# Strided sparse attention and a Mish MLP on one core: holding Pool's loads until the last transposed piece has landed, in every block

## The chip, the cores and the metric

The kernel runs on one core of one Trainium2 chip. The metric is device time in microseconds (us), lower is better. Before the change the median of three runs is 288.06 us (287.17 to 288.32).

## The reference

Attention over 8 batches of 8 heads, with 576 positions of 64 values, and then an MLP over all 4608 tokens. In four heads a position sees itself and the 31 positions before it (local); in the other four it sees the earlier positions that are congruent to it modulo 32 (strided).

```python
# q, k, v: 8 x 8 x 576 x 64 float32; w_in: 512 x 2048, w_out: 2048 x 512
scores = (q @ k.T) / sqrt(64)
rel = pos[:, None] - pos[None, :]
mask_local = (rel >= 0) & (rel < 32)                                   # heads 0 to 3
mask_strided = (rel >= 0) & (pos[None, :] % 32 == pos[:, None] % 32)   # heads 4 to 7
attn = softmax(where(mask, scores, -1e9))
x = (attn @ v)          # heads side by side: 4608 tokens x 512
h = x @ w_in
out = (h * tanh(softplus(h))) @ w_out
```

## The kernel before

**Blocks.** The 4608 tokens go through the MLP in nine blocks of 512 (t = 0 to 8), while attention goes by batch (576 tokens, b = 0 to 7). Block t computes the MLP of its 512 tokens and, woven into its second half, the attention of batch t+1; the attended tokens go into a ring `xT` of four batches. At the same time it brings in the data of batch t+2. The order on every engine is written out by hand: what is called first is queued first on its engine, and each engine works through its queue in order, waiting where an operand isn't there.

**One block** (t from 1 to 7). `mlp1` gives seven steps: `begin`, `second`, `third`, `fourth`, a group of matmuls, `fifth`, `end`. They form the first product and Mish, by a scheme with seven products of halves instead of eight. Then `mlp2_seven` gives 14 steps for the second product. After step i of these the list `at[i]` is called, with the attention of batch t+1:

- `at[0]`: `load_qk_str(t+2)`, the strided k and q of batch t+2 (tiles `ks`, `qs`), on Pool's queue.
- `at[1]`: the strided scores and the last part of the local scores (matmuls of line 333, which read the transposed `qTs`, `kTs`, `qTl`, `kTl`).
- `at[3]` and `at[5]`: masks of the local scores on Pool (line 353), the rest of the local scores, the first strided products with v.
- `at[7]`: ACT copies the rows of local v that neighbouring windows share (`share_v_loc`, line 181).
- `at[10]` to `at[12]`: the local products with v (line 369), and the transposes into `xT`.

**How a batch's q and k get transposed.** The strided ones are loaded by Pool's DMAs with a cast. The local ones come as float32 by SP's DMAs (`load_qk_loc`, line 140, tiles `kl32` and `ql32`), issued at the end of the block before, and Pool casts them after step 9 (`cast_qk_loc`, line 199). Then `transpose_by_dma(t+2)` queues six DMA transposes on SP after step 10: kTs, qTs (line 224), and kTl, qTl for each of two pairs of heads (line 230). The last is qTl of the second pair. They are used in the middle of the next block. Behind them on SP stand the two stores of the block's output (line 744), the DMA transposes of the tail of `xT` (line 445), and the next float32 loads.

**How v gets in.** Local v of batch t+1 is loaded in step `fourth` of block t by four DMAs on Pool's queue (`load_own_v_loc`, line 175, tile `vl`). Strided v of batch t+2 follows (`load_early_v_str`, line 154, tile `vsr`) and is spread by VectorE at the beginning of the next block. All of `load_own_v_loc`, `load_early_v_str` and `load_qk_str` are plain waits-and-issues in Pool's queue, so they stand one after the other there, behind the casts of the block before and ahead of the masks of this block.

**The mark.** In block 1 alone, Pool first copies four elements of the last transposed piece, `qTl[0:1, 1, S - 4:S]`, into a tile `mark` that nothing reads (line 628). Since the copy reads what the last DMA transpose writes, Pool waits there until that transpose has landed, and its loads are issued only then.

Of the kernel before, what the change touches and what calls it, by code (L numbers as in the profile page):

```python
# [43 lines left out]
def kernel(ctx, tc, q, k, v, moe_w_in, moe_w_out, out):  # L44
    nc = tc.nc
    B, H, S, D = q.shape
# [106 lines left out]
    def load_early_v_str(b):  # L153
        nc.gpsimd.dma_start(vs_raw(), v[b, 4:8].rearrange("h (p j) d -> p h (j d)", j=CS))
# [18 lines left out]
    def load_own_v_loc(b):  # L173
        for h in range(4):
            nc.gpsimd.dma_start(  # L175
                vl[b % 2][32:128, :, h, 0:D], v[b, h].rearrange("(w p) d -> p w d", p=WQ)
            )
# [328 lines left out]
    def mlp1(t, accs):  # L506
# [41 lines left out]
        def product(ps, f0, lhs, rhs, first=False, last=False):  # L548
            for n, p in enumerate(ps):
                for j in range(2):  # L550
                    f = f0 + 256 * n + 128 * j
                    for cc in range(2):
                        nc.tensor.matmul(  # L553
                            p[:, 256 * j:256 * j + 256], lhsT=lhs[:, cc, f:f + 128],
                            rhs=rhs[:, cc], start=(first and j == 0 and cc == 0),
                            stop=(last and cc == 1), skip_group_check=True,
                        )

        def mish(src, half_f, half_t, c0):
            src = src.rearrange("p (j n) -> p j n", n=256)  # L560
            c = 8 * half_f + c0
            nc.scalar.activation(  # L562
                gT[:, c:c + src.shape[1], 256 * half_t:256 * half_t + 256], src, AF.Mish,
            )
# [54 lines left out]
        def fourth():  # L619
            product(z[2], 0, a22, t4, last=True)  # L620
            for n in range(2):
                mish(z[2][n], 1, 0, 2 * n)
            if t == 1:
                sums_w()[2](slice(4, 8))
                sums_w()[3](slice(0, 4))
            sums_g(gT, 0, 4, "12")
            if t == 1:
                Po.tensor_copy(mark[:], qTl[0:1, 1, S - 4:S])
            if t < B - 1:
                load_own_v_loc(t + 1)  # L630
            if t < B - 2:
                load_early_v_str(t + 2)
# [9 lines left out]
        def end():  # L642
# [9 lines left out]
            sums_g(gT, 7, 8, "12")  # L652

        return gT, z, [begin, second, third, fourth, lambda: group(6), fifth, end]

    def sums(out_, in0, in1, op):
        nc.vector.tensor_tensor(out=out_, in0=in0, in1=in1, op=op)  # L657

    def sums_g(gT, c0, c1, which="1234"):

        lo1, lo2 = gT[:, c0:c1, 0:256], gT[:, c0:c1, 256:512]
        hi1, hi2 = gT[:, 8 + c0:8 + c1, 0:256], gT[:, 8 + c0:8 + c1, 256:512]
        s1, s2, s4 = [Sg[:, i, c0:c1, :] for i in range(3)]
        if "1" in which:
            sums(s1, lo2, hi2, ALU.add)
        if "2" in which:
            sums(s2, s1, lo1, ALU.subtract)
        if "3" in which:
            sums(lo2, lo1, lo2, ALU.subtract)
        if "4" in which:  # L670
            sums(s4, hi1, s2, ALU.subtract)
# [5 lines left out]
    def sums_w():  # L677

        b11, b12 = w_out[:, 0:8, 0:256], w_out[:, 0:8, 256:512]
        b21, b22 = w_out[:, 8:16, 0:256], w_out[:, 8:16, 256:512]  # L680
        return [
            lambda c: sums(tw_of(0)[:, c], b12[:, c], b11[:, c], ALU.subtract),
            lambda c: sums(tw_of(1)[:, c], b22[:, c], tw_of(0)[:, c], ALU.subtract),
            lambda c: sums(b12[:, c], b22[:, c], b12[:, c], ALU.subtract),
            lambda c: sums(tw_of(3)[:, c], b21[:, c], tw_of(1)[:, c], ALU.subtract),
        ]
# [364 lines left out]
```

## Time and profile before

| | before |
|---|---|
| median of 3 runs | 288.06 us (287.17 to 288.32) |
| profiled execution | 290.55 us |
| its span | 288.8 us |
| granted TensorE clock, mean | 0.993 |
| PE, PEld, DVE, ACT, POOL busy | 97%, 76%, 66%, 68%, 36% |
| DMA, mean over the span | 141 GB/s |

The span runs from the first to the last instruction of the profiled execution; its time holds some 1.75 us more around that. Busy shares are averages over the whole span, so the prediction cuts the span into blocks. PE is the matmul engine, PEld its weight loads, DVE VectorE, ACT ScalarE, POOL GpSimd, and SPq the queue of SyncE, which only issues DMAs. For an SPq row, the time is that of the issue; the landing is told separately. A DMA share above 1 means that packets of several queues were in flight on the same engines.

### The profile page before, as it was taken

The numbers are of one execution on the slowest core, as the hardware profiler recorded it, in microseconds if no ns is written. First come the engines' busy times: TensorE is split into PE (matmuls) and PEld (weight loads), VectorE is DVE, ScalarE is ACT, GpSimd is POOL, SyncE is SP. The second block draws the span as 40 slices with busy tenths as digits, with TensorE's granted clock in tenths as the row PEclk, the third lists the DMA queues.
The fourth block names the chain that finished last, engine by engine and source line by source line (L and its number), as shares of the span: only waits on it lengthen the run. The fifth ranks groups of instructions, "written<-read, shape, count | busy, mean of one in ns | idle before, by whom it ended". The sixth has DMA issues, their size and how long they took to land.

```text
span 288.8 us, 7515 instructions
## 1 busy us (share of the span) xinstructions
PE 279.3 (97%) x3106; PEld 219.3 (76%) x3121; DVE 190.8 (66%) x403; ACT 196.6 (68%) x292; POOL 105.3 (36%) x122
## 2 busy tenths in 40 slices
PE   8999999999999969999999999999999999999995
PEld 3564455686898648977898889778977897788684
DVE  2273167889786737768776777687868776735742
ACT  2578643699857947689758985898589858506920
POOL 8375536307396015910691069306710600000000
PEclk9999999999999979999999999999999999999999
DMA  8999999999979999999999999999993032003004
GB/s 158 185 205 190 193 194 199 145 137 241 171 102 116 130 257 160 144 235 152 161 109 123 218 151 139 143 227 151 160 149 113 1 137 47 0 3 145 0 2 145
DMA packets 103965, 40.73 MB, mean 141 GB/s; under 512 B 86396, under 2 KB 99436, under 8 KB 103932
## 3 DMA queue, kind: packets, MB, share of 16 engines
q1 hardware_dynamic: 67900, 25.13, 57.1%
q0 software_dynamic: 35744, 14.87, 46.8%
q8 instruction: 24, 0.39, 0.6%
q10 hardware_dynamic: 288, 0.25, 0.3%
q14 instruction: 9, 0.07, 0.1%
HBM read 37.20 MB, written 9.44 MB: 162 GB/s over the span
## 4 chain that ended last, share of the span: by engine, by line
PE 87%; DMA 7%; DVE 2%; ACT 1%; POOL 1%; issue 1%; SPq 0%; ACTq 0%; POOLq 0%
PE pso L749 30%; PE psu L553 10%; PE psh L522 9%; PE psv L553 8%; PE psb L553 7%; PE po L369 4%; PE pso L809 4%; PE psb L522 4%; PE pso L782 4%; DMA qTl<-ql 4%; DMA ql<-in_q_dram 4%; PE ps L333 3%; PE trx L418 1%; PE tr L267 1%; DVE x_l L381 1%
## 5 line engine op out<-in xcount | busy, mean ns | idle before, releaser
L353 POOL TENSOR_TENSOR Pl<-Pl,consts_sb 128x960 bf16<-128x960 bf16 (+1 forms) x18 | 29.2, 1635 | 87.1 <-issue 68.5
L749 PEld LDWEIGHTS <-gT 128*128 128x128 bf16 x448 | 41.8, 98 | 5.8
L553 PEld LDWEIGHTS <-w_in 128*128 128x128 bf16 x384 | 37.4, 98 | 8.5
L749 PE MATMUL pso<-w_out,gT 128*128 128x256 bf16 x336 | 40.9, 273 | 0.0
L749 PEld LDWEIGHTS <-Sg 128*128 128x128 bf16 x336 | 32.1, 100 | 5.1
L522 PEld LDWEIGHTS <-w_in 128*128 128x128 bf16 x208 | 20.3, 98 | 16.7 <-issue 0.6
L553 PEld LDWEIGHTS <-Sw 128*128 128x128 bf16 x288 | 28.2, 98 | 3.3
L522 PE MATMUL psh<-xT,w_in 128*128 128x512 bf16 (+1 forms) x127 | 29.0, 365 | 0.8 <-ACT xT L197 0.2
L749 PE MATMUL pso<-Tw,Sg 128*128 128x256 bf16 x224 | 28.0, 281 | 0.0
L197 ACT COPY xT<-trx 128x576 bf16<-128x576 bf16 (+3 forms) x24 | 14.2, 629 | 18.4 <-PE trx L418 13.0
L197 ACT COPY osb<-pso 128x512 f32<-128x512 f32 (+1 forms) x17 | 9.4, 554 | 22.3 <-PE pso L749 12.9
L562 ACT ACTIVATE gT<-psu 128x1024 bf16<-128x1024 f32 x16 | 16.4, 1025 | 8.4 <-PE psu L553 8.4
L657 DVE TENSOR_TENSOR psu<-psb,p 128x512 f32<-128x512 f32 x16 | 11.2, 700 | 13.8 <-PE psb L553 13.0
L395 DVE TENSOR_TENSOR x_s<-po,rden 72x512 bf16<-72x512 f32 x28 | 19.2, 687 | 1.0
L175 POOL DMA_DIRECT2D vl<-in_v_dram x24 | 18.8, 791 | 0.5 <-PE psv L553 0.4
L533 ACT ACTIVATE gT<-psh 128x1024 bf16<-128x1024 f32 x16 | 16.2, 1024 | 3.9 <-PE psh L522 3.8
L657 DVE TENSOR_TENSOR Sg<-gT 128x256 bf16<-128x256 bf16 (+2 forms) x32 | 12.8, 421 | 8.0 <-ACT gT L562 6.7
L553 PE MATMUL psu<-xT,w_in 128*128 128x256 bf16 x128 | 17.9, 272 | 0.0
L347 ACT ACTIVATE Ps<-ps 72x864 bf16<-72x864 f32 (+1 forms) x18 | 14.7, 857 | 4.6 <-PE ps L333 4.6
L726 DVE TENSOR_TENSOR p<-pso,p 128x512 f32<-128x512 f32 x14 | 9.6, 685 | 12.1 <-PE pso L749 12.1
L553 PE MATMUL psb<-Sx,w_in 128*128 128x256 bf16 x128 | 17.2, 272 | 0.0
L522 PE MATMUL psb<-xT,w_in 128*128 128x512 bf16 (+1 forms) x72 | 16.4, 355 | 0.0
(139 smaller groups left out, 593.2 us busy)
## 6 DMA issues: line engine op xcount, KB each, us to landing
out_dram<-osb SPq DMA_DIRECT2D x9, 512.0 KB, 8.0
out_dram<-p SPq DMA_DIRECT2D x7, 512.0 KB, 6.7
kl<-in_k_dram SPq DMA_DIRECT2D x5, 576.0 KB, 10.2
ql<-in_q_dram SPq DMA_DIRECT2D x5, 576.0 KB, 14.2
qs<-in_q_dram POOLq DMA_DIRECT2D x8, 288.0 KB, 13.4
vsr<-in_v_dram POOLq DMA_DIRECT2D x8, 288.0 KB, 9.4
w_in<-in_moe_w_in_dram POOLq DMA_DIRECT2D x4, 512.0 KB, 9.6
w_out<-in_moe_w_out_dram POOLq DMA_DIRECT2D x4, 512.0 KB, 17.9
```

Source lines behind the costliest of these rows:

```text
L175: nc.gpsimd.dma_start(vl[b % 2][32:128, :, h, 0:D], v[b, h].rearrange("(w p) d -> p w d", p=WQ))
L197: nc.scalar.copy(out_, in_)
L347: nc.scalar.activation(pt[0:n, :, 0:nw], ps[0:n, :, o0:o0 + nw], AF.Exp, scale=scale)
L353: meng.tensor_tensor(out=pm, in0=pm, in1=mk[0:n, :].unsqueeze(1).unsqueeze(1).to_broadcast([n, 2, nu, w]), op=ALU.mult,)
L369: nc.tensor.matmul(po[:, h, :], lhsT=pt[0:n, c0:c0 + 128], rhs=rhs, start=True, stop=True,)
L395: nc.vector.tensor_tensor(out=dst.rearrange("p e (h d) -> p e h d", h=4), in0=po[0:m, :, :, 0:D], in1=rden[0:m].unsqueeze(3).to_broadcast( ...
L522: nc.tensor.matmul(ps_u[:, o:o + n], lhsT=w_in[:, cc, fc * 128:(fc + 1) * 128], rhs=xT[:, cc, a:a + n], start=(cc == 2 and (o == 0 or len( ...
L533: nc.scalar.activation(to, tiles[g][:], AF.Mish)
L553: nc.tensor.matmul(p[:, 256 * j:256 * j + 256], lhsT=lhs[:, cc, f:f + 128], rhs=rhs[:, cc], start=(first and j == 0 and cc == 0), stop=(la ...
L562: nc.scalar.activation(gT[:, c:c + src.shape[1], 256 * half_t:256 * half_t + 256], src, AF.Mish,)
L657: nc.vector.tensor_tensor(out=out_, in0=in0, in1=in1, op=op)
L749: nc.tensor.matmul(ps[:, pair, :], lhsT=lhs(c, 128 * pair), rhs=rhs(c), start=(first and pair == 0 and c == 0), stop=(last and c == 7), sk ...
```

## The change

The copy into `mark`, and with it the wait for the last transposed piece, is done in every block in which local v is loaded (t = 1 to 6), not only in block 1. The loads themselves, their order and their sizes are the same.

```diff
             sums_g(gT, 0, 4, "12")
-            if t == 1:
+            if t < B - 1:
                 Po.tensor_copy(mark[:], qTl[0:1, 1, S - 4:S])
-            if t < B - 1:
                 load_own_v_loc(t + 1)
             if t < B - 2:
                 load_early_v_str(t + 2)
```

## The prediction

> **What bounds the kernel now.** I read the page first, then the busy time of the seven steady blocks (stretches cut where PE starts a block's first product), then the waits, the chain, and the Pool and SP queues in order of time.
>
> ```profile
> span 288.8 us, 7515 instructions
> PE 279.3 (97%) x3106; PEld 219.3 (76%) x3121; DVE 190.8 (66%) x403; ACT 196.6 (68%) x292; POOL 105.3 (36%) x122
> ...
> 57.40:86.46 29.06, 29.01 (x350) 24.40 (x349) 24.97 (x50) 24.23 (x36) 14.34 (x16) 1.00 1.24 162
> 86.46:119.90 33.44, 30.72 (x349) 25.26 (x349) 21.49 (x44) 23.40 (x35) 13.92 (x16) 0.95 1.36 164
> 119.90:148.88 28.98, 28.93 (x347) 24.30 (x347) 21.42 (x44) 23.02 (x35) 13.13 (x15) 1.00 1.27 166
> 148.88:177.81 28.93, 28.93 (x362) 25.79 (x361) 21.41 (x44) 22.88 (x35) 12.60 (x14) 1.00 1.43 158
> 177.81:206.71 28.90, 28.85 (x346) 24.21 (x345) 21.51 (x44) 22.86 (x35) 12.12 (x14) 1.00 1.40 163
> 206.71:235.51 28.80, 28.75 (x343) 24.14 (x343) 21.93 (x44) 22.70 (x35) 8.87 (x9) 1.00 0.58 99
> ...
> PE ps L333 <- DMA qTl<-ql: 2.7, 2, 1.5
> ...
> 93.96 10.47 DMA qTl<-ql
> ```
>
> The columns of a stretch are its length, the busy time of PE, PEld, DVE, ACT and POOL, the granted clock, the DMA share and GB/s. These are blocks 1 to 6. PE sets the time: blocks 3 to 6 are 28.8 to 29.0 us of PE without a gap. Only block 2 is longer, 33.44 us. Against block 3 that is **4.46 us**: PE is idle for 2.72 us (33.44 less 30.72) instead of 0.05, and busy 1.79 us longer under a granted clock of 0.95. The wait row and the chain name the cause: the score matmuls L333 waited 2.7 us for transposed pieces of q, the last of which was issued at 93.96 and landed 10.47 us later, at 104.43. So a DMA wait of PE costs 4.46 / 2.67 = 1.67 times its length here. The other blocks have no PE time to win; they can only lose.
>
> **What the change removes.** Block 1 has the hold already, block 2 doesn't. The two show what company does to the last transpose.
>
> ```profile
> L230 SPq DMA_TRANSPOSE qTl<-ql x1: 1210/1210/1210, 62.7 to 62.7; - x1
> DMA to landing us min/median/max: 3.0/3.0/3.0
> ...
> L230 SPq DMA_TRANSPOSE qTl<-ql x1: 2812/2812/2812, 94.0 to 94.0; - x1
> DMA to landing us min/median/max: 10.5/10.5/10.5
> ...
> 65.84 0.71 POOL L628 COPY mark<-qTl 1x4 bf16<-1x4 bf16 x1 [11.46 <-DMA qTl<-ql]
> 66.50 0.72 POOL L175 DMA_DIRECT2D vl<-in_v_dram  x1
> 70.64 0.72 POOL L126 DMA_DIRECT2D ks<-in_k_dram  x1
> 71.35 0.70 POOL L126 DMA_DIRECT2D qs<-in_q_dram  x1
> 85.77 3.25 POOL L175 DMA_DIRECT2D vl<-in_v_dram  x4
> ...
> 50.99 1.44 SPq L224 DMA_TRANSPOSE kTs<-ks  x1
> 84.00 1.44 SPq L224 DMA_TRANSPOSE kTs<-ks  x1
> 85.84 1.78 SPq L224 DMA_TRANSPOSE qTs<-qs  x1
> 206.12 1.22 SPq L230 DMA_TRANSPOSE kTl<-kl  x1
> 210.07 1.25 SPq L230 DMA_TRANSPOSE qTl<-ql  x1
> ```
>
> With Pool's loads held the last piece landed in 3.0 us, with four vl loads and more started at 85.77 it took 10.5. Held in block 2 too, the six transposes (one DMA each for kTs and qTs, two each for kTl and qTl) start at 84.00 as before and run alone. Their length alone is in no row. Low: kTs and qTs are issued by 85.84 + 1.78 = 87.6, four local pieces take 3.95 us from first to last issue (206.12 to 210.07), the last lands in 3.0: 94.6, or 10.6 us. High: the set of 50.99 to 65.84, 14.8 us, whose issues were spaced wider. I take 11.5, nearer to the low row, because block 2's casts are done when Pool goes on to vl at 85.77; the landing is then 95.5. The score matmuls need the last piece 15.2 us into a block (row 163.42 below, from 148.88), that is at 101.7. **Block 2's loss goes: 4.46 us in the profiled execution.** That execution took 290.55 us with a span of 288.8, 1.75 around it; the median of the shown runs is 288.06, 2.49 less. If all of that lies in block 2's wait, the gain in an ordinary run is 4.46 - 2.49 = 1.97. I keep 1.97 and 4.46 as its ends and sum with 4.46.
>
> The Trainium skill, page "DMA: Bandwidth & Descriptors", section "Queues, rings and completion order", says that each DMA engine takes turns between the queues that have work, packet by packet. An estimate by that page: two queues sharing evenly double a transfer, so block 2's set of 20.4 us in company would take 10.2 alone and every cycle below would be 1.3 us shorter; the traced 3.0 against 10.5 is worse than double, so I don't build on it.
>
> **What it adds.** Per block one 0.71 us copy on Pool, and a wait in front of it. Queued behind it on Pool are four vl loads, one vsr load (block 6: vl alone), ks and qs, and behind those the masks of the local scores and the casts of kl and ql. Nothing is behind it on SP. The wait is never free: the last transpose needs the ql cast that stands just ahead of the mark on the same queue.
>
> ```profile
> 137.57 0.91 POOL L353 TENSOR_TENSOR Pl<-Pl,consts_sb 128x384 bf16<-128x384 bf16 x1 [13.66 <-issue]
> 140.67 3.96 POOL L353 TENSOR_TENSOR Pl<-Pl,consts_sb 128x960 bf16<-128x960 bf16 x2 [2.19 <-ACT Pl L347]
> 163.42 0.71 PE ps L333 x36
> 171.85 1.26 ACT L181 COPY vl<-vl 32x1280 bf16<-32x1280 bf16 x1
> 173.56 0.42 PE L369 MATMUL po<-vl,Pl 128*128 128x65 bf16 x8
> ...
> L175 POOL DMA_DIRECT2D vl<-in_v_dram x4: 725/725/734, 66.5 to 69.2; - x4
> DMA to landing us min/median/max: 6.8/7.1/9.8
> ...
> L126 POOL DMA_DIRECT2D ks<-in_k_dram x1: 720/720/720, 70.6 to 70.6; - x1
> DMA to landing us min/median/max: 13.3/13.3/13.3
> ...
> L175 POOL DMA_DIRECT2D vl<-in_v_dram x4: 725/762/815, 207.7 to 210.0; - x4
> DMA to landing us min/median/max: 5.5/6.0/6.7
> ...
> 98.53 3.95 SPq L445 DMA_TRANSPOSE xT<-x_l  x2
> 185.18 5.77 SPq L445 DMA_TRANSPOSE xT<-x_l  x4
> ```
>
> Call m the landing of the last piece. *Masks.* Pool has issued all loads 72.05 - 65.84 = 6.2 us after m; its first mask is due 17.7 us into a block (137.57 from 119.90), so up to m = +11.5 (11.5 us into its block) the 13.66 us of idle time cover the delay. Beyond that two masks (0.91 + 1.98) must end by +24.7, where local PV starts (173.56 from 148.88): m up to +15.6. *Local v.* In block 1 the slowest vl landing is bounded by 66.50 + 9.8 = 76.3, m + 10.5. ACT then shares rows (1.26 us) before PV at +24.7, so vl must be there at +23.4: **m up to +12.9**, tighter than the scores' +15.2. In block 6, with less to load, the limit is 23.4 - (0.7 + 2.3 + 6.7) = +13.7.
>
> *The next set.* ks is issued 4.8 us after m, lands 13.3 later, and only then does SP start the next set: 84.00 - 65.84 = 18.2 us from m in block 1. So the hold closes a loop: m, loads, landing, transposes, next m. Its length is 18.2 + 11.5 = 29.7 us, plus what the transposes of xT cost, which block 1 doesn't send. Two took SP's queue 3.95 us, four 5.77; bounds are 0 and their mean, 4.9; local pieces, leaving SP every 1.3 us, suggest less than half of that, and I take 2.0. **Cycle: 31.7 us against a block of 28.9.** Ends: 28.8 (10.6 and 0) and 37.9 (14.8 and 4.9).
>
> *The sum.* Blocks start at 86.46, then (less 4.46) 115.44, 144.42, 173.35, 202.25. m is 95.5 (+9.0), 127.2 (+11.8), 158.9 (+14.5, 1.6 too late, times 1.67 = 2.7 us); block 5 then starts at 176.05, m is 190.6 (+14.55, costs 2.75); block 6 starts at 207.7, m is 222.3 (+14.6, 0.9 too late, costs 1.5). Lost 6.95, won 4.46: **+2.5 us, 290.6 us** on the median.
>
> **The rivals.**
>
> *Faster: the work of the DMA engines is only reordered.* Before, last pieces still landed well in most blocks, and the DMA share of 1.27 to 1.43 in blocks 3 to 5 says that the engines were busy in company anyway. If the transposes run so much faster alone that they give back what the loads lose, the cycle stays at or below 30.1, m in block 6 is at or below 215.9 (+13.7) and no block waits. The gain is 1.97 to 4.46, 283.6 to 286.1; I put it at 284.6. It decides at a cycle of 30.1, only 0.4 above the sum without xT. The Trainium skill, "DMA: Bandwidth & Descriptors", section "Issuing engines are not separate DMA queues", speaks for it: all queues run on the same 16 engines and interleave. Against it stands the gap that the hold leaves, 18.2 us in which no transpose can start.
>
> *Cancelled out.* At a cycle of 31.3 the same working loses 1.3 + 3.1 + 0.6 = 5.0 and wins 4.46: within 0.5% of before. About 30.9 to 31.5 gives this; 288.
>
> *Much slower.* At a cycle of 33, m is +13.1, +16.8, +14.4, +16.0: lost 0.25 + 6.5 + 2.5 + 3.8 = 13.0, net +8.6, 296.6. For it: xT's 3.95 to 5.77 us on SP stand whole in the cycle.
>
> That the hold does nothing can be left out, by the order of cast and mark on Pool.
>
> **How the numbers follow.** The cycle decides: 0.32 for the reorder, 0.14 for cancelled out, 0.40 for the forecast, 0.14 for much slower. A measurement here can tell about 0.5%, 1.44 us. So faster 0.32, same 0.14, slower 0.54. The range goes from 284.4, into the reorder's gain, to 296.0, short of the far case; the forecast's own range is 289.5 to 294.
>
> **What would show it.** In the profile after: block 2 is 29 us, its last qTl lands in 3 to 5 us near 95.5, and the mark starts there; marks follow at distances of about 31.7 us; SP's kTs transposes start about 18 us after each mark; in blocks 4 to 6 ACT's L181 or PE's L369 waits for vl, in the later ones perhaps L333 for qTl as well. Marks every 30 us or less, each under 12.9 us into its block, and blocks of 28.9 throughout would prove me wrong, as would vl loads that land within 7 us after the mark.

## Result and the profile after

The changed kernel takes 286.81 us (median of six runs, 286.68 to 287.23), the kernel before 288.19 in the same comparison (287.17 to 288.96): a ratio of **0.9954, 95% interval 0.9932 to 0.9977**. It is faster by 1.4 us, where 2.5 us slower was forecast. In a second comparison the ratio was 0.9962 (0.9929 to 0.9994). The ratios leave out executions that lie more than 1.5% above the fastest of their kernel, which here only kernels had whose profiles show PE waiting; medians and ranges in this text are over all executions.

The profiled execution took 286.68 us with a span of 284.8, 4.0 less than the span before. The same cut into blocks 1 to 6 as in the prediction (columns as there):

```profile
57.55:86.60 29.05, 29.05 (x350) 24.38 (x349) 24.95 (x50) 24.24 (x36) 13.65 (x15) 1.00 1.23 168
86.60:115.67 29.07, 29.07 (x351) 24.40 (x349) 21.50 (x44) 23.18 (x35) 12.73 (x15) 1.00 1.24 169
115.67:144.65 28.98, 28.98 (x348) 24.32 (x347) 21.89 (x44) 23.02 (x35) 13.41 (x15) 1.00 1.17 163
144.65:173.58 28.93, 28.93 (x362) 25.78 (x361) 22.22 (x44) 22.88 (x35) 13.01 (x15) 1.00 1.32 159
173.58:202.47 28.89, 28.89 (x347) 24.20 (x345) 22.76 (x44) 22.86 (x35) 13.80 (x15) 1.00 1.22 166
202.47:231.28 28.81, 28.81 (x345) 24.16 (x343) 21.41 (x44) 22.70 (x35) 9.61 (x10) 1.00 0.71 113
```

Block 2 is 29.07 us, 4.37 less than in the profile before. PE is busy for the whole of every block and its clock is 1.00 throughout; the waits of PE for qTl are gone, and no new one has come. Pool's queue shows the marks, and the ks load behind the first of them; SP's queue shows the starts of the next sets, and the last load of ql ahead of one of them:

```profile
65.98 0.72 POOL L628 COPY mark<-qTl 1x4 bf16<-1x4 bf16 x1 [10.47 <-DMA qTl<-ql]
70.76 0.72 POOL L126 DMA_DIRECT2D ks<-in_k_dram  x1
94.33 0.18 POOL L628 COPY mark<-qTl 1x4 bf16<-1x4 bf16 x1 [9.04 <-DMA qTl<-ql]
122.37 0.18 POOL L628 COPY mark<-qTl 1x4 bf16<-1x4 bf16 x1 [5.90 <-DMA qTl<-ql]
151.70 0.18 POOL L628 COPY mark<-qTl 1x4 bf16<-1x4 bf16 x1 [5.84 <-DMA qTl<-ql]
182.03 0.18 POOL L628 COPY mark<-qTl 1x4 bf16<-1x4 bf16 x1 [6.03 <-DMA qTl<-ql]
212.87 0.18 POOL L628 COPY mark<-qTl 1x4 bf16<-1x4 bf16 x1 [7.11 <-DMA qTl<-ql]
```

```profile
83.16 1.34 SPq L224 DMA_TRANSPOSE kTs<-ks  x1
109.25 3.43 SPq L224 DMA_TRANSPOSE kTs<-ks  x1
137.30 5.47 SPq L224 DMA_TRANSPOSE kTs<-ks  x1
165.86 7.36 SPq L224 DMA_TRANSPOSE kTs<-ks  x1
188.86 7.81 SPq L140 DMA_DIRECT2D ql<-in_q_dram  x1
196.78 6.55 SPq L224 DMA_TRANSPOSE kTs<-ks  x1
```

The marks come 28.35, 28.04, 29.33, 30.33 and 30.84 us after one another, 29.4 on average and growing towards the end, against the forecast 31.7. They start 8.4, 7.7, 6.7, 7.1, 8.5 and 10.4 us into their blocks; the limits worked out in the prediction are 12.9 and 13.7. From a mark to the next set's first transpose it is 17.2 us in block 1, close to the 18.2 of before the change, but then only 14.9, 14.9, 14.2 and 14.8. From there to the next mark it is 11.2, 13.1, 14.4, 16.2 and 16.1.

The last piece of block 2, and the ks loads of blocks 2 and 5, by the groups of these tiles:

```profile
L230 SPq DMA_TRANSPOSE qTl<-ql x1: 1225/1225/1225, 91.6 to 91.6; - x1
DMA to landing us min/median/max: 2.6/2.6/2.6
...
L126 POOL DMA_DIRECT2D ks<-in_k_dram x1: 757/757/757, 98.5 to 98.5; - x1
DMA to landing us min/median/max: 10.7/10.7/10.7
...
L126 POOL DMA_DIRECT2D ks<-in_k_dram x1: 754/754/754, 186.2 to 186.2; - x1
DMA to landing us min/median/max: 9.6/9.6/9.6
```

Without Pool's loads beside it, the last transpose lands in 2.6 us instead of 10.5, at 94.2. And ks, which the prediction let land in 13.3 us in every block, takes 10.7 in block 2 and 9.6 in block 5. In block 5 ks is there at 195.8, but SP comes to kTs only when the issue of ql ends, at 196.7: there SP's own queue closes the loop, 0.9 us later.

### The profile page after: what moved, and what is told of

The parts are those of the page before. It is cut to its first block, busy times and chain, and to the rows that moved or that the text cites. A ratio compares the mean times of both kernels' runs of the same rounds, so it can differ in the third digit from the quotient of the medians.

```text
span 284.8 us, 7535 instructions
## 1 busy us (share of the span) xinstructions
PE 279.0 (98%) x3121; PEld 218.6 (77%) x3121; DVE 193.0 (68%) x403; ACT 196.4 (69%) x292; POOL 106.3 (37%) x127
## 4 chain that ended last, share of the span: by engine, by line
PE 92%; DMA 2%; DVE 2%; ACT 1%; issue 0%; ACTq 0%; POOLq 0%
PE pso L748 31%; PE psu L553 10%; PE psh L522 10%; PE psv L553 9%; PE psb L553 8%; PE psb L522 5%; PE po L369 4%; PE pso L808 4%; PE pso L781 4%; PE ps L333 4%; DMA ks<-in_k_dram 2%; PE trx L418 1%; PE un L281 1%; PE tr L267 1%; PE tr L253 1%; DVE x_s L395 1%
## 5 line engine op out<-in xcount | busy, mean ns | idle before, releaser
L748 PEld LDWEIGHTS <-Sg 128*128 128x128 bf16 x336 | 31.5, 98 | 4.4
L522 PE MATMUL psh<-xT,w_in 128*128 128x512 bf16 (+1 forms) x136 | 29.4, 366 | 0.2 <-ACT xT L197 0.2
L197 ACT COPY xT<-trx 128x576 bf16<-128x576 bf16 (+3 forms) x24 | 14.2, 629 | 18.4 <-PE trx L418 13.0
L748 PE MATMUL pso<-Tw,Sg 128*128 128x256 bf16 x224 | 26.7, 273 | 0.0
L197 ACT COPY osb<-pso 128x512 f32<-128x512 f32 (+1 forms) x17 | 9.4, 555 | 20.2 <-PE pso L748 10.8
L562 ACT ACTIVATE gT<-psu 128x1024 bf16<-128x1024 f32 x16 | 16.4, 1025 | 8.4 <-PE psu L553 8.4
L656 DVE TENSOR_TENSOR psu<-psb,p 128x512 f32<-128x512 f32 x16 | 11.2, 700 | 11.8 <-PE psb L553 11.0
L533 ACT ACTIVATE gT<-psh 128x1024 bf16<-128x1024 f32 x16 | 16.2, 1024 | 4.0 <-PE psh L522 3.9
L175 POOL DMA_DIRECT2D vl<-in_v_dram x24 | 17.8, 751 | 2.0 <-issue 1.5
L656 DVE TENSOR_TENSOR Sg<-gT 128x256 bf16<-128x256 bf16 (+2 forms) x32 | 12.8, 422 | 8.0 <-ACT gT L562 6.7
L628 POOL COPY mark<-qTl 1x4 bf16<-1x4 bf16 x6 | 1.6, 268 | 44.4 <-DMA qTl<-ql 44.4
L553 PE MATMUL psb<-Sx,w_in 128*128 128x256 bf16 x128 | 17.2, 272 | 0.0
## 6 DMA issues: line engine op xcount, KB each, us to landing
ql<-in_q_dram SPq DMA_DIRECT2D x5, 576.0 KB, 16.4
```

Source lines behind the costliest of these rows:

```text
L175: nc.gpsimd.dma_start(vl[b % 2][32:128, :, h, 0:D], v[b, h].rearrange("(w p) d -> p w d", p=WQ))
L197: nc.scalar.copy(out_, in_)
L522: nc.tensor.matmul(ps_u[:, o:o + n], lhsT=w_in[:, cc, fc * 128:(fc + 1) * 128], rhs=xT[:, cc, a:a + n], start=(cc == 2 and (o == 0 or len( ...
L533: nc.scalar.activation(to, tiles[g][:], AF.Mish)
L553: nc.tensor.matmul(p[:, 256 * j:256 * j + 256], lhsT=lhs[:, cc, f:f + 128], rhs=rhs[:, cc], start=(first and j == 0 and cc == 0), stop=(la ...
L562: nc.scalar.activation(gT[:, c:c + src.shape[1], 256 * half_t:256 * half_t + 256], src, AF.Mish,)
```

## Experiments

In every comparison the kernel before was timed beside the others.

**The kernel before, again.** No edit.

> The kernel before, unchanged, run again: how much of the wait in block 2 belongs to one execution. Theory A (the wait for qTl in block 2 is there in every execution, and is longer in some than in others): a ratio of 1.000 within 0.3%, and the profiled execution again has a block 2 that is 1 to 4.5 us longer than block 3. Rival (the 4.46 us were an accident of that one profiled execution, and ordinary ones lose nothing there): block 2 is within 0.3 us of block 3 in this profile.

Ratio 1.0019 (0.9982 to 1.0056); twelve executions from 286.5 to 293.6 us, median 288.56. Blocks 2 and 3 of its profiled execution, which took 288.03 us:

```profile
86.45:116.85 30.40, 29.24 (x350) 24.55 (x349) 21.50 (x44) 23.39 (x35) 13.21 (x15) 1.00 1.36 158
116.85:145.83 28.98, 28.98 (x348) 24.32 (x347) 21.42 (x44) 23.00 (x35) 12.76 (x14) 1.00 1.40 171
```

Block 2 has the wait again, but loses only 1.42 us (30.40 against 28.98), 1.16 of it idle, under a clock of 1.00. So the rival falls: the 4.46 us were no accident of one execution, but a long case with a clock that fell. That the wait is there in every execution, as theory A says, isn't shown: the shortest one, 286.53 us, is as short as the shortest of the changed kernel (286.57) and leaves hardly any room for a loss of 1.4.

**Holds in blocks 1 and 2 alone**, twice. The edit is shown against the changed kernel.

```diff
-            if t < B - 1:
+            if t in (1, 2):
                 Po.tensor_copy(mark[:], qTl[0:1, 1, S - 4:S])
+            if t < B - 1:
                 load_own_v_loc(t + 1)
```

> The hold in blocks 1 and 2 only. Theory A (all of the gain is block 2's wait for qTl, the holds of blocks 3 to 6 are neutral because the loads keep enough time): 286.5 to 287.2 us, as with the hold in every block, and blocks 3 to 6 stay at 28.8 to 29.0 us. Rival B (one hold only moves the wait: without a hold in block 3 the transposes meet the loads again there or in block 5): block 3, 4 or 5 is longer than 29.5 us and the time is 287.8 to 289.

> The hold in blocks 1 and 2 only, again, beside a hold in blocks 1, 2 and 5: the first time its median was 287.3, with some executions at 288.8 to 290.2, which the changed kernel did not have. Theory A2 (without a hold the last piece of block 5 lands 13 us into the block with only 2 us to spare, and in some executions later than its use): median 287.0 to 287.8, some executions near 289, and if the profiled execution is one of these, its block 5 is longer than 28.9 and L333 waits there for qTl. Rival (blocks 3 to 6 never wait, the first time was chance): all executions within 286.5 to 287.6.

The first time: median 287.32 (286.64 to 290.18), ratio to before 0.9999 (0.9959 to 1.0039). The second time: 286.91 (286.41 to 288.55), ratio 0.9934 (0.9901 to 0.9968). The first shows no gain, within 0.4%; the second is the whole gain. The two ran on different chips, and the changed kernel was not beside the first. In both profiles PE waits for no DMA in blocks 2 to 6; blocks 3 to 5 of the second are these:

```profile
115.99:144.97 28.98, 28.98 (x348) 24.32 (x347) 21.41 (x44) 23.02 (x35) 12.94 (x15) 1.00 1.41 171
144.97:173.90 28.93, 28.93 (x362) 25.77 (x361) 21.57 (x44) 22.88 (x35) 13.29 (x15) 1.00 1.38 179
173.90:202.83 28.93, 28.93 (x347) 24.14 (x345) 21.51 (x44) 22.86 (x35) 13.29 (x15) 1.00 1.41 165
```

A hold in block 2 was enough for the gain the second time; the first time that isn't shown. That blocks 3 to 6 wait in some executions, theory A2, no profile showed either, but they come close: without a hold in block 3 its last piece was issued at 121.27 and 119.23 and landed in 9.1 and 10.8 us, 14.1 and 14.0 us into the block; in the kernel before, run again, it landed 14.9 us in (119.95 + 11.8, from 116.85). PE uses it at 15.2. Where the four executions of 288.85 to 290.18 lost their time the first time stays open.

**Holds in blocks 1, 2 and 5.** The edit is the same with `(1, 2, 5)`.

> Holds in blocks 1, 2 and 5. Theory A2: as the changed kernel, 286.5 to 287.3 us with hardly an execution above 288. Rival (the late executions come from blocks 3, 4 or 6): median and spread as with holds in 1 and 2.

286.65 us (286.45 to 289.34), three of twelve above 288; ratio 0.9954 (0.9916 to 0.9992). The median is that of the change; the late executions are not fewer than the one of twelve that holds in 1 and 2 had beside it. It doesn't tell A2 from its rival.

**Holds everywhere but in block 2; no hold at all.** The condition is `t in (1, 3, 4, 5, 6)`, and then the copy is left out.

> The hold in blocks 1 and 3 to 6, not in block 2. Theory A: as before the change, 287.8 to 288.6 us, with a wait for qTl in block 2 and none elsewhere. Rival B (the holds of blocks 3 to 6 bring or cost something of their own): below 287.3, or above 289 because the set after block 2's stall is late.

> No hold in any block; block 1's is taken out too. Theory A (a hold pays where the set starts late, which is where few microseconds lie between its issue and its use): block 1's set is issued as late as block 2's, so its last piece lands some 10 us after issue instead of 3.0, near 73, after its use at 72, and block 1 waits 1 to 3 us; block 2's own set then starts earlier, since its loads were not held, and it may wait less. 287.5 to 290 us. Rival B (the hold of block 1 is what makes block 2 late, and costs more than it brings): below 287.0, no wait in either block.

Without block 2's hold: median 288.50 (286.68 to 292.93), ratio 0.9981 (0.9947 to 1.0015). Without any: 289.11 (286.43 to 293.69), ratio 0.9983 (0.9946 to 1.002). By their ratios neither can be told from the kernel before, and both keep its long tail. Where the wait sits is seen in their profiles, of executions of 291.33 and 292.89 us. These are long ones: they show where a long execution waits, not what an ordinary one loses. First blocks 2 and 3 without block 2's hold, then blocks 1 and 2 without any, with the wait row of that one:

```profile
86.76:120.38 33.62, 30.90 (x351) 25.45 (x349) 22.22 (x44) 23.39 (x35) 15.35 (x16) 0.95 1.32 169
120.38:149.36 28.98, 28.98 (x348) 24.32 (x347) 21.42 (x44) 23.00 (x35) 13.27 (x15) 1.00 1.23 165
```

```profile
57.60:93.05 35.45, 31.41 (x350) 25.72 (x348) 25.00 (x50) 24.35 (x36) 11.43 (x13) 0.90 1.35 154
93.05:122.12 29.07, 29.07 (x351) 24.39 (x349) 21.51 (x44) 23.16 (x35) 13.22 (x15) 1.00 1.19 165
...
PE ps L333 <- DMA qTl<-ql: 4.0, 1, 4.0
```

Without block 2's hold the wait is back in block 2, and in no other. Without block 1's hold block 1 has the wait, longer (4.0 us) than the 1 to 3 that were expected, and in this profile block 2 is clean without a hold. Theory A had that: a set of transposes that starts late needs the hold. In this profile block 2's set starts at 79.12, 13.9 us ahead of its block, against 84.00, 2.5 us ahead, before the change. Of these 11.4 us some 4.9 are the earlier start of the set (with nothing held in block 1, ks is issued at 59.74 instead of 70.64); the rest is block 1's own wait, which makes block 2 start late.

**The changed kernel, again.**

> The changed kernel, run again beside the others: is the spread of the executions, not only their median, what the hold changes? Before, executions ranged from 286.5 to 290.9 us among those compared, and with holds in blocks 1 and 2 alone four of twelve still took 288.8 to 290.2. Theory A (the holds of blocks 3 to 6 take away waits that come only in some executions): all twelve within 286.5 to 287.6 us. Rival (blocks 3 to 6 are neutral, and the spread comes from the stretch before block 1 or from the chip): as with holds in blocks 1 and 2, some executions at 288.5 to 290.

286.89 us (286.57 to 288.15); eleven of twelve lie within 286.57 to 287.37. The kernel before, beside it, ran from 286.51 to 291.79. The best executions are as good before as after; what the change takes away are the long ones. Theory A missed by one execution.

**Pool's loads 2 and 4 us later.** Memsets of a tile that is no longer used, behind the mark.

```diff
                 Po.tensor_copy(mark[:], qTl[0:1, 1, S - 4:S])
+                for _ in range(7 if t > 1 else 0):     # 14 in the second
+                    Po.memset(gate[:], 0.0)
```

> Seven memsets of a tile that is no longer used stand on Pool behind each mark of blocks 2 to 6, about 2 us; the loads are issued that much later. Theory A (a closed loop: mark, ks issued, ks landed, next transposes, next mark, as the prediction had it, but of 28 to 31 us): marks later by 0, 2, 4, 4 to 6, 6 to 8 us in blocks 2 to 6, so 7.7, 8.7, 11, 13 and 17 us into their blocks; vl becomes late in blocks 5 and 6 and the time goes up by 3 to 8 us. Rival C (the loop is not closed by ks: SP's own queue of stores, xT transposes and float32 loads decides when the next set starts): marks move by less than 1 us in every block and the time stays at 286.8.

> The same with fourteen memsets, about 4 us. Theory A: marks later by 0, 4, 8, 12, 16 us unless PE is held up and lets them catch up, the vl loads miss the sharing copy on ACT from block 3 or 4 on, each late block costs 2 us or more; 294 to 302 us. Rival C: marks move by less than 2 us, vl lands 4 us later and still in time, 286.8 to 287.5.

With 2 us more: 287.15 us (286.35 to 289.25), ratio to before 0.9955 (0.9921 to 0.9989). Its marks, with the waits that are new:

```profile
95.32 0.18 POOL L628 COPY mark<-qTl 1x4 bf16<-1x4 bf16 x1 [9.64 <-DMA qTl<-ql]
125.63 0.58 POOL L628 COPY mark<-qTl 1x4 bf16<-1x4 bf16 x1 [7.53 <-DMA qTl<-ql]
157.54 0.20 POOL L628 COPY mark<-qTl 1x4 bf16<-1x4 bf16 x1 [11.91 <-DMA qTl<-ql]
186.61 0.18 POOL L628 COPY mark<-qTl 1x4 bf16<-1x4 bf16 x1 [8.65 <-DMA qTl<-ql]
218.60 0.24 POOL L628 COPY mark<-qTl 1x4 bf16<-1x4 bf16 x1 [6.43 <-DMA qTl<-ql]
...
ACT vl L181 <- DMA vl<-in_v_dram: 3.5, 3, 2.1
PE po L369 <- ACT vl L181: 1.6, 2, 1.2
...
115.86:145.38 29.52, 29.14 (x348) 24.39 (x347) 23.03 (x44) 23.00 (x35) 17.57 (x24) 1.00 1.05 158
145.38:175.85 30.47, 29.24 (x362) 25.88 (x361) 21.80 (x44) 22.86 (x35) 14.04 (x21) 1.00 1.01 159
```

The marks of blocks 2 to 6 come 1.0, 3.3, 5.8, 4.6 and 5.7 us later than with the change (8.5, 9.8, 12.2, 10.8 and 13.8 us into their blocks). So rival C falls, and the loop that the prediction described is closed: up to block 4 the delay adds up. It doesn't stay a full 2 us per round, though. In block 5 it gets smaller, and from block 2 to 6 a round, from mark to mark, takes 30.8 us on average, 1.2 more than with the change (29.6). The wait that comes first is the one that the prediction named: ACT's copy of the shared rows waits for vl, and PE's local product for that copy. Block 3 loses 0.5 us and block 4 1.5 in this profile, and the clock stays at 1.00. In blocks 5 and 6, which theory A named, PE doesn't wait, although block 6's vl loads are issued only 16.4 us into the block (221.19 from 204.75): they land in 3.8 to 4.5 us. Theory A's 3 to 8 us are too much: the median goes up by 0.3.

With 4 us more: 296.01 us, the median of four executions (291.05, 295.75, 296.26 and 297.44). Blocks 2, 3 and 5 of the one of 296.26 are 31.19, 32.68 and 33.05 us long:

```profile
86.54:117.73 31.19, 29.54 (x350) 24.49 (x349) 22.58 (x44) 23.16 (x35) 18.77 (x31) 1.00 1.07 155
117.73:150.41 32.68, 30.87 (x348) 25.61 (x347) 21.71 (x44) 23.10 (x35) 17.55 (x29) 0.95 1.04 152
179.34:212.39 33.05, 30.97 (x347) 25.52 (x345) 21.68 (x44) 22.94 (x35) 18.05 (x29) 0.95 0.99 152
```

Three of the four are within theory A's 294 to 302, the fourth is below. With 2 us more the first waits show and the median hardly moves, with 4 every execution takes at least 4 us more: the change lies some 2 us away from the point from which a hold costs.

**The float32 loads of local k and q ahead of the stores on SP.**

```diff
                     at[10].append(lambda: transpose_by_dma(t + 2))
+                    if t < B - 3:
+                        at[10].append(lambda: load_qk_loc(t + 3))
...
-            if t < B - 3:
+            if t == 0:
                 load_qk_loc(t + 3)
```

> On SP's queue the float32 loads of the next local k and q stand directly behind the six transposes, ahead of the two stores and of the xT transposes (blocks 2 to 5; in block 1 as before). Pool's held loads then run against them from the start, as they did in block 1. Theory A (ks landed in 9.6 to 10.7 us instead of the predicted 13.3 because the float32 loads come 3 to 6 us later than in block 1): ks lands in 12 us or more, the next set starts later, the cycle of the marks grows by 1 to 2 us; the marks of blocks 5 and 6 are 12 us or more into their blocks; time 286.8 to 290. Rival D (ks lands earlier for another reason, the float32 loads do not matter): ks lands within 0.7 us of 10.7 and 9.6, marks as with the change.

289.15 us (287.64 to 292.51), within theory A's 286.8 to 290, ratio to before 1.0013 (0.9973 to 1.0052). ks in blocks 2 and 4, Pool's marks from block 3 on, and the new waits:

```profile
L126 POOL DMA_DIRECT2D ks<-in_k_dram x1: 745/745/745, 99.2 to 99.2; - x1
DMA to landing us min/median/max: 13.2/13.2/13.2
...
L126 POOL DMA_DIRECT2D ks<-in_k_dram x1: 757/757/757, 158.1 to 158.1; - x1
DMA to landing us min/median/max: 14.9/14.9/14.9
...
125.15 0.18 POOL L628 COPY mark<-qTl 1x4 bf16<-1x4 bf16 x1 [10.74 <-DMA qTl<-ql]
153.94 0.35 POOL L628 COPY mark<-qTl 1x4 bf16<-1x4 bf16 x1 [10.46 <-DMA qTl<-ql]
184.24 0.24 POOL L628 COPY mark<-qTl 1x4 bf16<-1x4 bf16 x1 [11.74 <-DMA qTl<-ql]
214.13 0.53 POOL L628 COPY mark<-qTl 1x4 bf16<-1x4 bf16 x1 [11.47 <-DMA qTl<-ql]
...
DVE x_l L395 <- DMA xT<-x_l: 4.4, 2, 2.2
PE psu L553 <- DVE x_l L395: 1.7, 2, 0.9
```

In blocks 2 to 5 ks lands in 12.8 to 14.9 us again, 2.5 to 5.0 later than with the change: the place of the float32 loads on SP does set it, and rival D falls. But the cycle hardly grew. Its marks, from 66.15 on, are 28.8, 30.2, 28.8, 30.3 and 29.9 us apart, 29.6 on average against 29.4; theory A's 1 to 2 us more are missed, and so are marks at 12 us. What ks loses, the transposes win: from SP's first transpose (112.43, 142.57, 173.07 and 201.25 in this profile's SP queue) to the mark it took 12.7, 11.4, 11.2 and 12.9 us, with no float32 load beside them (those landed by 103.2, 133.3 and 165.5), against 13.1 to 16.2 with the change. The time was lost elsewhere: VectorE waited 2.2 us, twice, for xT transposes to finish reading `x_l`, and PE waited for VectorE, 1.7 us in all.

**Local v not held.** `load_own_v_loc(t + 1)` stands ahead of the copy.

> The four loads of local v stand ahead of the mark in blocks 1 to 6; only strided v, q and k are held. Theory A: company of any kind slows the transposes, but 0.6 MB of vl is a fourth of the held loads, so the last piece of blocks 1 and 2 lands in 4 to 7 us instead of 2.6 to 3.0 and 10.5; marks 1 to 3 us later; no PE wait, 286.7 to 287.5. Rival E (the vl loads alone are what slows the transposes, they are the first in line): the last piece of block 2 lands in 9 us or more and PE waits there as before the change; 287.8 to 289.

286.91 us (286.69 to 287.55), ratio 0.9936 (0.9905 to 0.9967). The last pieces of blocks 1 and 2 landed in 6.6 and 5.7 us. PE waits for no transpose. Theory A holds in landing and time: a fourth of the load slows the transpose by part of the way, not enough for PE to wait. The marks aren't 1 to 3 us later throughout, as it had it: by the two profiles they come 4.1 us later in block 1, 1.7 in block 2, within 0.5 in blocks 3 and 4 and 1.2 and 1.8 earlier in blocks 5 and 6.

## Why the prediction was wrong

**Right: what block 2 loses and why.** Its wait for qTl came from the loads beside transposes that start late, and is gone. The last piece landed at 94.2 (forecast 95.5) in 2.6 us. Block 2 is 4.37 us shorter, of the forecast 4.46, and the whole span 4.0.

**Right: that an ordinary execution gains less.** The prediction gave 1.97 as the low end, and even that was too much; measured are 1.4. An ordinary loss should have been the value of the sum: the other profile of the kernel before lost 1.42 us in that block.

**Wrong: the term for xT, and with it the cycle.** The step that failed reads "Cycle: 31.7 us against a block of 28.9". 29.4 was measured. The first two terms alone, 18.2 + 11.5 = 29.7, come within 0.3 of that; to them the prediction added 2.0 for the transposes of xT, because SP's queue spends 4 to 6 us on them. With the float32 loads in block 1's order and all xT transposes sent, a round took 17.0 to 19.1 us from a mark to the next set and 11.2 to 12.9 from there to the next mark, 29.6 in all. So by this comparison xT's cost in the cycle is near 0, the low end of the given bounds; no run leaves the xT transposes out. The loop waits for Pool's loads during that time, and SP's xT work runs beside them. In the changed kernel the two terms are not those of the prediction: with xT ahead of the float32 loads ks lands earlier, and the transposes take longer instead (14.2 to 14.9 and 13.1 to 16.2 from block 2 on). So 29.7 fits the changed kernel only because two errors of some 3 us cancel, which the prediction had not foreseen: that is luck.

What that does to the sum: at a cycle of 29.7 the prediction's own working puts the marks 9.8, 10.5, 11.3 and 12.1 us into blocks 3 to 6, all below the limits. The loss of 6.95 us was then nothing. The rival "the work of the DMA engines is only reordered" had the mechanism: what the loads lose the transposes give back (from the first issue to the last landing a set took 18.5 to 23.7 us in blocks 2 to 5 before, and 11.2 to 16.2 after), the cycle is below its deciding 30.1 on average (the last two rounds, 30.3 and 30.8, are not), and no block waits. Its 283.6 to 286.1 us was too low, since it too counted on at least 1.97. The measured number lies where "cancelled out" had put its own, but by another way: no wait eats the gain. The Trainium skill, "DMA: Bandwidth & Descriptors", section "Issuing engines are not separate DMA queues", which was cited for the rival, says that the DMAs of all issuing engines run on the same 16 DMA engines and interleave. The runs agree: another order on SP's queue moves the landing of Pool's ks by 2.5 to 5.0 us, and the cycle by 0.2.

**Too tight: the limits.** They let the slowest vl load take 9.8 us, as in block 1. With the change the slowest landed 5.1 to 6.7 us after its issue in blocks 2 to 6, so that vl was there at most 7.8 to 9.4 us after the mark instead of 10.5, and the mark could have come 1 to 2.7 us later than the prediction let it.

**Wrong: the price of a short wait.** The factor 1.67 was taken from a wait of 2.72 us after which the clock fell, to 0.95 over the block. Waits of 1.16 us (before, again) and of 1.23 (block 4 with 2 us more on Pool, 30.47 less 29.24) left it at 1.00, and cost 1.42 and 1.54 us, their length and 0.3. When the clock falls the extra cost is no share of the wait either: it is about 2 us (last section).

**Shown by the delays: the loop.** That later loads make the next mark later, and that vl on its way to ACT's copy is what is late first, came as described. That a round passes on only part of a delay, 1.2 of 2 us, was not foreseen.

**Open.** Why PE's wait in block 2 is 2.7 us in one execution and 1.2 in another (the rest of the 3 us between them is the clock), and where holds in blocks 1 and 2 alone lost up to 3 us in a few. That the holds of blocks 3 to 6 bring something isn't shown: with holds in 1 and 2, or 1, 2 and 5, eight of 36 executions took more than 288 us, with all holds one of 18, and such counts don't decide it. The 0.2 to 1.2 us to spare in block 3 without a hold leave it possible.

## What to carry to other kernels

When a loop through several queues is costed, don't add a term for work that another queue does while the loop waits anyway: look whether the queue that does it is the one that the loop waits for. A delay that adds up decides by tenths per round. So when a term that no row shows may be 0, and the sum without it stands on the other side of the deciding value (here 29.7, below 30.1), give both sides nearly even chances. And where ordinary runs are faster than the profiled one, part of the loss that the profile shows isn't there to be won.

## What the runs showed of the hardware

These lengths are taken against the same block of the changed kernel. Where PE stood idle for 1.2 us, the block took 1.3 to 1.5 us longer and the clock stayed at 1.00. With 1.65 us idle (block 2 with 4 us more on Pool) it took 2.1 longer, still at 1.00. In five blocks with 1.8 us idle or more the clock was 0.95 or 0.90, and beside the idle time PE was busy 1.7 to 2.4 us longer: 2.7 us idle and 1.7 or 1.8 more (block 2 before, and in the kernel without block 2's hold), 4.0 and 2.4 (block 1 without any hold), 1.8 and 1.9, 2.1 and 2.1 (blocks 3 and 5 with 4 us more). So the extra depends little on the length of the wait. It comes at the end of the wait: in the profile before, PE's wait in block 2 ends at 104.5, the clock is 0.50 from 104 to 107 us, and over these two stretches of 5 us the lower clock costs, by an estimate from the shares 0.80 and 0.86, 1.0 and 0.7 us:

```profile
101.00:106.00 5.00, 2.33 (x43) 1.72 (x40) 2.34 (x4) 2.95 (x7) 0.00 (x0) 0.80 1.22 268
106.00:111.00 5.00, 5.00 (x67) 4.16 (x66) 2.75 (x6) 1.61 (x3) 0.90 (x1) 0.86 1.34 208
```

The idle times are sums over a block and can lie in several gaps, in block 2 before of 1.46 and 1.21 us.

The last DMA transpose of a set landed in 2.6 to 3.4 us with Pool's loads held, in 4.5 to 6.6 with only the four vl loads ahead of it, and in 5.0 to 14.9 with none of the loads held. In the last case it was mostly longer the further ahead of it the first vl load was issued. In blocks 3, 4, 5 and 2 before the change that was 2.1, 2.8, 4.1 and 8.2 us, and the transpose took 5.3, 7.9, 10.1 and 10.5; in block 1 without any hold it was 7.4 us, and 14.9. So a landing of 10 us is not special to block 2. What is special there is that the last piece is issued 7.5 us into the block (4.3 in the second profile), against 3.5 or less in blocks 3 to 5, and that it is needed at 15.2.
